# Grams over four banks, a split first substitution and a ranked routing in a delta rule with experts

## The chip, the cores and the metric

One core of a Trainium2 chip runs the whole program. TensorE (PE) multiplies, ScalarE (ACT) and VectorE (DVE) evict PSUM and do elementwise work, GpSimd (POOL) does elementwise work and issues indirect DMAs, SyncE (SP) issues the other DMAs. The metric is the device time of one execution in microseconds (us).

## What is computed

For 4 batches and 8 heads a linear attention with the delta rule runs over 768 tokens with heads of 48; its output, 384 wide per token, goes through a gated layer of 8 experts, one per token, in which a token may keep the expert of the token before it:

```python
for t in range(S):
    kt, vt, bt = (k_n[:, :, t], v[:, :, t], beta[:, :, t, None])
    y[:, :, t] = np.einsum('bhd,bhde->bhe', q[:, :, t], state)
    v_old = np.einsum('bhde,bhd->bhe', state, kt)
    state = state + bt[:, :, :, None] * np.einsum('bhd,bhe->bhde', kt, vt - v_old)
...
    fresh_e = int(np.argmax(logits[b, s]))
    if s == 0 or local_gate[b, s] < 0.5:
        e = fresh_e
    else:
        e = prev_e if prev_e >= 0 else fresh_e
...
    h = np.maximum(x[b, s] @ w1[e], 0.0)
    out[b, s] = p[e] * (h @ w2[e])
```

k_n is the normalised key; the 3072 tokens are spread over the experts by a routing that depends on the data.

## The kernel before

The attention is done in 12 chunks of 64 tokens, n = 0 to 11, two of which make a macro, m = 0 to 5. For each chunk K(n) loads keys and queries (KQ, four DMAs) and multiplies them on TensorE: four products (operand half g, bank c), each into a bank of the two-bank pool pt, each evicted by two ScalarE operations (gt, G) and two of VectorE (gt, amp). For each macro T_(m) transposes gt into L (L218), forms the norms and the factors mu (L220 to L226, one square root on ScalarE), writes mu on the diagonal of X (L231), scales L in two halves (L232) and solves a triangular system by forward substitution: 31 steps j, each of two operations (fg, the product of column j of L with row j of X, L241; X less that, L242) on 31-j rows by j+1 columns. A table SPLIT gives, for each macro, how many columns VectorE does; in the kernel before it is zero everywhere, so all steps run on GpSimd. The result X is transposed to TT (L249) and TX (L252). Per chunk, Tc(n) then makes the matrix XT from TT and TX (two small products through pt, four ScalarE copies), and online(n) does what depends on the state S: kps<-S, R (L288, VectorE), kps<-R,xtp, Us (L300), the new state Sps, S (L307), the output y through yps (ScalarE L312, VectorE L313), its store to xs and its DMA transpose xt, and the logits of 64 tokens (TensorE L326, VectorE L330).

The experts' part begins inside this: the weights of expert 0 are loaded early. A first routing (z=0) takes 20 of 24 pieces of the tokens, up to chunk 9, and gathers a lot of 256 tokens of expert 0; a second (z=1) waits for chunk 11 and completes the positions. Then come expert 0's up- and down-projections for both lots, expert 1, and, in an order written by hand (rest), experts 2 to 7, with weights split in a high and a low f16 part (low part: line 433, method `lo` of weights, L457 to L474). A down-projection (downm, L451) takes 24 matmuls of 384 columns for each tile of up to 128 tokens.

The order of everything up to expert 2 comes from a list scheduler, Sched: each operation has an engine or a choice of engines, a cost, and a rank that is the longest path behind it; `boost` adds to the rank, `links` add a path that isn't a dependence. Operations with `claim` wait for other operations on the same buffer as a whole. What the scheduler puts on an engine runs in that order; an instruction that waits holds up all behind it on its engine.

## Time and profile before

| | |
|---|---|
| median of 3 runs | 582.48 us (582.31 to 582.53) |
| profiled execution | 586.47 us, of which the span 584.8 |
| TensorE busy | 459.1 us, 79% of the span |
| VectorE busy | 329.3 us, 56% |
| GpSimd busy | 285.9 us, 49%, of which the substitution 109.8 + 98.4 |
| ScalarE busy | 210.6 us, 36% |

The shares are means over stages. Up to about 267 us the substitutions run on GpSimd, from about 360 us the experts on TensorE; between them lie the last two chunks and the two routings. The share of the whole span therefore says little about a change; the stretch in which it lies says more. A row of a timeline gives the start, the duration, the engine, the line of the kernel, the operation, its output and inputs, how many instructions the row joins, and in brackets how long the engine was idle before it and who released it.

### The profile page before, as it was taken

The numbers are of one execution on the slowest core, as the hardware profiler recorded it, in microseconds if no ns is written. First come the engines' busy times: TensorE is split into PE (matmuls) and PEld (weight loads), VectorE is DVE, ScalarE is ACT, GpSimd is POOL, SyncE is SP. The second block draws the span as 40 slices with busy tenths as digits, with TensorE's granted clock in tenths as the row PEclk, the third lists the DMA queues.
The fourth block names the chain that finished last, engine by engine and source line by source line (L and its number), as shares of the span: only waits on it lengthen the run. The fifth ranks groups of instructions, "written<-read, shape, count | busy, mean of one in ns | idle before, by whom it ended". The sixth has DMA issues, their size and how long they took to land. (4 is left out here: it accounts for less than half of the span.)

```text
span 584.8 us, 18802 instructions
## 1 busy us (share of the span) xinstructions
PE 459.1 (79%) x8119; PEld 351.9 (60%) x8119; DVE 329.3 (56%) x722; ACT 210.6 (36%) x346; POOL 285.9 (49%) x492
## 2 busy tenths in 40 slices
...
GB/s 224 215 188 1 0 3 58 161 46 129 165 106 106 142 147 165 86 112 57 4 110 244 79 157 94 117 179 48 123 200 126 171 172 174 152 213 151 90 13 25
DMA packets 63668, 69.47 MB, mean 119 GB/s; under 512 B 42931, under 2 KB 54255, under 8 KB 63584
## 3 DMA queue, kind: packets, MB, share of 16 engines
...
HBM read 49.49 MB, written 10.05 MB: 102 GB/s over the span
## 5 line engine op out<-in xcount | busy, mean ns | idle before, releaser
L242 POOL TENSOR_TENSOR X<-X,fg 128x31 f32<-128x31 f32 (+15 forms) x186 | 109.8, 590 | 14.6
L241 POOL TENSOR_TENSOR fg<-L,X 128x31 f32<-128x31 f32 (+15 forms) x186 | 98.4, 529 | 16.0 <-DVE X L231 1.6
L167 PE MATMUL pt<-W 48*64 48x128 f32 x768 | 64.1, 374 | 22.6 <-DVE gt L210 13.6
L167 PEld LDWEIGHTS pt<-W 48*64 48x64 f32 x768 | 55.3, 193 | 27.3 <-DVE gt L210 16.3
L448 PEld LDWEIGHTS <-W 128*128 128x128 f16 x432 | 43.7, 102 | 33.4 <-issue 6.9
L448 PE MATMUL pt<-kv,W 128*128 128x384 f16 (+3 forms) x288 | 61.5, 346 | 0.9 <-DVE ft L450 0.7
L450 DVE TENSOR_SCALAR ft<-pt 128x384 f32<-128x384 f32 (+6 forms) x72 | 40.1, 557 | 22.6 <-ACT W L449 14.6
L167 PE MATMUL pt<-TT,G 32*32 32x32 f32 x768 | 24.3, 229 | 31.8 <-DVE TT L249 30.8
L211 DVE TENSOR_TENSOR amp<-pt,mask 128x256 f32<-128x256 f32 x48 | 20.2, 422 | 50.1 <-ACT gt L208 30.9
L449 ACT ACTIVATE W<-pt 128x256 f16<-128x256 f32 (+4 forms) x28 | 12.2, 437 | 85.5 <-PE pt L448 84.1
L167 PEld LDWEIGHTS pt<-TT,G 32*32 32x32 f32 x768 | 22.5, 139 | 33.0 <-issue 27.2
L433 DVE SCALAR_TENSOR_TENSOR W<-W,W 128x768 f16<-128x768 f32 (+1 forms) x33 | 35.9, 1093 | 10.1 <-ACT W L431 9.9
L455 PEld LDWEIGHTS <-W 128*128 128x128 f16 (+2 forms) x272 | 28.0, 103 | 21.9 <-issue 6.4
...
L436 POOL DMA_INDIRECT G<-xs,gi x25 | 26.6, 1066 | 22.2 <-PE pt L612 12.6
L167 PE MATMUL kps<-R,xtp 64*64 64x48 f32 x704 | 35.6, 281 | 0.7 <-issue 0.7
L449 ACT ACTIVATE xtp<-pt 128x384 f16<-128x384 f32 (+4 forms) x28 | 14.7, 526 | 56.0 <-PE pt L448 43.9
L167 PEld LDWEIGHTS kps<-R,xtp 64*64 64x64 f32 x704 | 34.4, 200 | 0.9 <-issue 0.7
L431 ACT ACTIVATE W<-W 128x768 f16<-128x768 f32 (+1 forms) x33 | 30.2, 935 | 10.7 <-DMA W<-in_moe_w_dram 8.2
L208 ACT ACTIVATE gt<-pt,ma 128x128 f32<-128x128 f32 x48 | 22.4, 479 | 27.1 <-PE pt L167 18.6
...
L455 PEld LDWEIGHTS <-amp 128*128 128x128 f16 (+2 forms) x224 | 22.6, 101 | 14.6 <-issue 0.9
(307 smaller groups left out, 944.1 us busy)
## 6 DMA issues: line engine op xcount, KB each, us to landing
...
G<-xs,gi POOLq DMA_INDIRECT x25
kv<-G SPq DMA_TRANSPOSE x25
```

Of the source, the lines that this page charges most:

```text
L167: mm=lambda o,l,r,st,sp,tp:MM(o,l,r,start=st,stop=sp,skip_group_check=True,tile_position=tp)
L208: add(lambda go=go,gv=gv:nc.scalar.activation(go(),gv()[:,:,0:32],AF.Copy,scale=s.ma[:,0:1]),r=[ps,"mask"],w=[key],claim=[gt],e='A',c=ca(128))
L211: add(lambda gv=gv,n0=n0:nc.vector.tensor_tensor(am.t[:,n0:n0+4,:],gv()[:,:,64:128],s.mask.unsqueeze(1).to_broadcast([128,4,64]),op=ALU.mu ...
L241: eng.tensor_tensor(tv,l[:,j,j+1:].unsqueeze(2).to_broadcast([128,n,k]),x[:,j,x0:x1].unsqueeze(1).to_broadcast([128,n,k]),op=ALU.mult)
L242: eng.tensor_tensor(x[:,j+1:,x0:x1],x[:,j+1:,x0:x1],tv,op=ALU.subtract)
L431: if e in (None,s.nc.scalar): s.nc.scalar.mul(o,i,256.0)
L433: def wlo(s,st,w,k): s.nc.vector.scalar_tensor_tensor(s.wv(w,k)[:,1],s.wst(st,k),256.0,s.wv(w,k)[:,0],op0=ALU.mult,op1=ALU.subtract)
L436: return s.nc.gpsimd.indirect_dma_start(out=x[0:m],out_offset=None,in_=s.xs[0:nt,:],in_offset=bass.IndirectOffsetOnAxis(ap=ix[0:m],axis=0) ...
L448: for k in range(3): s.nc.tensor.matmul(ps,s.wv(W[k],k)[:,a,0,128*f:128*f+128],xT[:,3*b+k,:],start=(x==0 and k==0),stop=(x==2 and k==2))
L449: def uphi(s,h,ps): s.nc.scalar.activation(h,ps,AF.Relu,scale=2.0**-6)
L450: def upt(s,t,ps): s.nc.vector.tensor_scalar(t,ps,0.0,2.0**-6,op0=ALU.max,op1=ALU.mult)
L455: s.nc.tensor.matmul(po[0:m],h(a,f)[:,c:c+m],s.wv(W[k],k)[:,b,f%2,:],start=(x==0 and f==0),stop=(x==2 and f==7))
```

## The change

- SPLIT becomes 4 for macro 0: columns 0 to 3 of its substitution go to VectorE (temporary fv), GpSimd starts at step 4 with columns 4 and up. The costs of the steps and one link of the planner change.
- The grams of chunks 0 and 1 go into kps and yps (two banks each), 16 matmuls in one operation. A one-element GpSimd copy (`held`) waits for chunk 1's keys; the loads of later keys and of all values wait for it.
- The routing's 12 small VectorE constants come behind the scaling of macro 0 in the program.
- Tc copies the lower half of XT in one 128-partition operation, and it and the masked copy may go to VectorE.
- Tc and online of chunk n get a rank raised by 2000 (12-n); grams of later chunks are linked to earlier evictions.
- The first routing gets a rank raised by 20000.
- Low parts 3 to 6 of expert 1's weights are put on GpSimd.
- The last tiles of at most 64 tokens use down2: two halves of 192 columns in two column groups of TensorE.
- L and X tiles join the pool of weight buffers; further costs in the planner change.

```diff
-    NKV=3; NW=15; NAMP=6; NXT=3; NLX=2; NGT=1; NUS=2; SPLIT=(0,0,0,0,0,0)
+    NKV=3; NW=15; NAMP=6; NXT=3; NLX=2; NGT=1; NUS=2; SPLIT=(4,0,0,0,0,0)
...
-        for f,e,c in extra: add(f,e=e,c=c,w=["consts"])
...
+                k1=ch[1]["KQ"][1]; add(lambda:nc.gpsimd.tensor_copy(KQ[0].t[0:1,0,0:1],k1.t[0:1,0,0:1]),r=[k1],w=[KQ[0]],e='G',c=200); s.held=S.ops[-1]
...
+                if n<2:
+                    bb=(s.pkp,s.pyp)[g](); bt_=bb.pool.tiles[0]; pc=[bt_[:,0],bt_[:,1]]
+                    def f(g=g,pc=pc):
                         k=KV(KQ[g].t)
                         for u in range(4):
...
+                            for j,c,q in H: mm(pc[c][B(q),128*u:128*u+128],k[D(j),u,q,0,:],k[D(j),u,q].rearrange("r z t -> r (z t)"),u==0,True,(64*j,64*q))
+                    add(f,r=[KQ[g]],w=[(bb,0),(bb,1)],claim=[bb,gt,am,G2],e='P',c=1300)
...
-                    add(fm,r=[(L,j//16)],w=[(X,p),("fm",p)],claim=[L,X],e='VG'[p],c=400+2.4*n*k if p==0 else 450+3.5*n*k)
+                    add(fm,r=[(L,j//16)],w=[(X,p),("fm",p)],claim=[L,X],e='VG'[p],c=300+3.2*n*k if p==0 else 590+3.85*n*k)
...
+            add(lambda e:(e.copy if e is nc.scalar else e.tensor_copy)(XT.t[:,:,32:64],tt()),r=[TT],w=[(XT,1)],claim=[XT],e='AV',c=dict(A=1070,V=700))
             for q in range(2):
-                o,o2=slice(64*q,64*q+32),slice(64*q+32,64*q+64)
-                add(lambda o2=o2:nc.scalar.copy(XT.t[o2,:,32:64],tt()[o2]),r=[TT],p=[XT],e='A',c=ca(512))
...
+                if m<0:
+                    for f,e,c in extra: add(f,e=e,c=c,w=["consts"]); S.ops[-1].pre.update([s.scaled] if e=='V' else ())
...
+                    i0=len(S.ops); Tc(n); online(n)
+                    for o in S.ops[i0:]: o.boost=2000.*(N-n)
...
+    def down2(s,po,h,W,c,m,y,pv):
+
+        for f in range(8):
+            k=3+f//2
+            for x,(a,b) in enumerate(((0,0),(0,1),(1,0))):
+                for g in range(2):
+                    s.nc.tensor.matmul(po[64*g:64*g+m,0:192],h(a,f)[:,c:c+m],s.wv(W[k],k)[:,b,f%2,192*g:192*g+192],start=(x==0 and f==0),stop=(x==2 and f==7),skip_group_check=True,tile_position=(0,64*g))
+        s.nc.scalar.copy(y[0:m,192:384],po[64:64+m,0:192])
+        s.nc.vector.tensor_scalar(y[0:m,0:192],po[0:m,0:192],pv[0:m],2.0**-26,op0=ALU.mult,op1=ALU.mult)
+        s.nc.vector.tensor_scalar(y[0:m,192:384],y[0:m,192:384],pv[0:m],2.0**-26,op0=ALU.mult,op1=ALU.mult)
...
-            add(lo,r=[CK,w],w=[st],p=[(w,'lo')],claim=[w],e='VG',c=dict(V=cv(n),G=2*cg(n))); S.ops[-1].pre.update(aft[1:] if aft else ())
+            add(lo,r=[CK,w],w=[st],p=[(w,'lo')],claim=[w],e='G' if aft and k>2 else 'VG',c=dict(V=cv(n),G=2*cg(n))); S.ops[-1].pre.update(aft[1:] if aft else ())
...
+            if z==0:
+                for o_ in S.ops[iz_:]: o_.boost=2e4
...
+                if m>64:
+                    s.downm(po,lambda z,f:h(z,f,n),W[e],range(8),128*j,m); s.yo(y,po,s.pv[:,a:a+1],m)
+                else: s.down2(po,lambda z,f:h(z,f,n),W[e],128*j,m,y,s.pv[:,a:a+1])
```

What the planner makes of it is seen at three places. The first is VectorE at the end of macro 1's transposes (L_118 and X_120 belong to macro 1, L_117 and X_119 to macro 0). Before, the mu chain and the scaling of L follow at once:

```order
L218 STREAM_TRANSPOSE L_118<-gt_112 128x256 x4
L220 TENSOR_SCALAR ss_109<-L_118 128x32
L222 RECIPROCAL t_111<-s_110 128x32
L224 TENSOR_TENSOR t_111<-t_111,ss_109 128x32
L224 TENSOR_TENSOR t_111<-t_111,s_110 128x32
L224 TENSOR_SCALAR nn_105<-t_111 128x32
L224 RECIPROCAL mm_108<-nn_105 128x32
L226 TENSOR_TENSOR t_111<-mm_108,bt_104 128x32
L226 TENSOR_TENSOR mm_108<-mm_108,t_111 128x32
L232 TENSOR_TENSOR L_118<-L_118,mm_108 128x512
L231 COPY X_120<-mm_108 128x32
```

After, the same chain is interrupted behind its first operations by the columns of macro 0 (fv), of which the first of 26 steps stand here,

```order
L233 STREAM_TRANSPOSE L_118<-gt_112 128x256 x4
L235 TENSOR_SCALAR ss_109<-L_118 128x32
L256 TENSOR_TENSOR fv<-L_117,X_119 128x104
L257 TENSOR_TENSOR X_119<-X_119,fv 128x26x4
L237 RECIPROCAL t_111<-s_110 128x32
L256 TENSOR_TENSOR fv<-L_117,X_119 128x100
L257 TENSOR_TENSOR X_119<-X_119,fv 128x25x4
```

and goes on only behind the last of them:

```order
L256 TENSOR_TENSOR fv<-L_117,X_119 128x4
L257 TENSOR_TENSOR X_119<-X_119,fv 128x4
L243 STREAM_TRANSPOSE nT_106<-nn_105 128x32
L239 TENSOR_TENSOR t_111<-t_111,ss_109 128x32
L239 TENSOR_TENSOR t_111<-t_111,s_110 128x32
L239 TENSOR_SCALAR nn_105<-t_111 128x32
L239 RECIPROCAL mm_108<-nn_105 128x32
L241 TENSOR_TENSOR t_111<-mm_108,bt_104 128x32
L241 TENSOR_TENSOR mm_108<-mm_108,t_111 128x32
L247 TENSOR_TENSOR L_118<-L_118,mm_108 128x512
L246 COPY X_120<-mm_108 128x32
```

So the scaling of macro 1's L, the last operation here but one, moved behind 52 operations of macro 0.

The second place is VectorE at the end of macro 5 (TT and TX are the transposes of its X, R that of chunk 10, y_135 the output of chunk 9). Before:

```order
L276 TENSOR_TENSOR kv_102<-kv_102,nT_107 128x768
L249 STREAM_TRANSPOSE TT_121<-X_120 128x256 x4
L252 STREAM_TRANSPOSE TX_122<-X_120 128x256 x4
L288 TENSOR_TENSOR R_131<-kv_101,kps 128x768
L313 SCALAR_TENSOR_TENSOR y_135<-yps,y_135 128x2x384
L330 COPY lg<-pt_147 128x18
```

After:

```order
L328 SCALAR_TENSOR_TENSOR y_135<-yps,y_135 128x2x384
L303 TENSOR_TENSOR R_131<-kv_101,kps 128x768
L264 STREAM_TRANSPOSE TT_121<-X_120 128x256 x4
L267 STREAM_TRANSPOSE TX_122<-X_120 128x256 x4
L285 COPY xtp_99<-TT_121 128x16x32
L273 TENSOR_SCALAR xtp_99<-TT_121,ma 128x16x32
L345 COPY lg<-pt_146 128x18
L345 TENSOR_TENSOR lg<-lg,pt_146 128x18
L345 TENSOR_SCALAR lg<-lg 128x18
L536 TENSOR_REDUCE mxl<-lg 128x20
```

R and y moved ahead of the transposes that wait for GpSimd's last step, and the first routing (L536) follows the next logits.

The third place is GpSimd behind its last substitution step (hz and G are gathers of tokens). Before:

```order
L242 TENSOR_TENSOR X_120<-X_120,fg 128x31
L436 DMA hz_128<-xs,gi 128x768
L436 DMA hz_129<-xs,gi 128x768
L657 COPY oh<-oh_209 128x8x20
L657 COPY oh<-oh_211 128x8x4
L661 TENSOR_TENSOR y_135<-oh,ps 128x192
L436 DMA G_113<-xs,gi 128x768
L436 DMA G_114<-xs,gi 128x768
```

After:

```order
L687 COPY oh<-oh_211 128x8x4
L691 TENSOR_TENSOR y_135<-oh,ps 128x192
L499 TENSOR_TENSOR X_120<-X_120,c_168 128x768
L499 TENSOR_TENSOR W_83<-X_120,W_83 128x768
L499 TENSOR_TENSOR W_84<-W_84,c_168 128x768
L499 TENSOR_TENSOR xtp_97<-W_84,xtp_97 128x768
L499 TENSOR_TENSOR xtp_98<-xtp_98,c_168 128x768
L499 TENSOR_TENSOR xtp_99<-xtp_98,xtp_99 128x768
L499 TENSOR_TENSOR amp_91<-amp_91,c_168 128x768
L499 TENSOR_TENSOR amp_92<-amp_91,amp_92 128x768
L454 DMA G_113<-xs,gi 128x768
L454 DMA G_114<-xs,gi 128x768
```

Eight operations on expert 1's weights (L499, 128x768) now stand ahead of the gathers into G.

## Rows read from the trace of the kernel before

**Rows 1.** Busy time of each engine (and its instructions), granted TensorE clock, DMA, by stretch:
```profile
core 0: us, PE busy (x) PEld busy (x) DVE busy (x) ACT busy (x) POOL busy (x), PEclk, DMA share, GB/s
270.00:285.00 15.00, 13.84 (x455) 13.29 (x452) 1.92 (x5) 8.99 (x13) 0.00 (x0) 0.50 0.32 56
315.00:330.00 15.00, 4.49 (x71) 3.52 (x70) 13.51 (x38) 6.22 (x8) 2.15 (x2) 0.50 0.25 86
360.00:570.00 210.00, 201.37 (x1236) 117.60 (x1234) 136.83 (x229) 66.28 (x103) 51.27 (x43) 1.00 0.46 134
```

**Rows 2.** Timeline of GpSimd, ends of macros: start, duration (us), operation, count, [idle <-releaser]:
```profile
28.65 0.52 POOL L241 TENSOR_TENSOR fg<-L,X 128x31 f32<-128x31 f32 x1
...
68.49 0.24 POOL L241 TENSOR_TENSOR fg<-L,X 128x31 f32<-128x31 f32 x1
...
226.20 0.53 POOL L241 TENSOR_TENSOR fg<-L,X 128x31 f32<-128x31 f32 x1 [1.39 <-DVE X L231]
...
267.08 0.25 POOL L242 TENSOR_TENSOR X<-X,fg 128x31 f32<-128x31 f32 x1
```

**Rows 3.** Timeline of GpSimd, single operations of macro 0:
```profile
47.96 0.62 POOL L241 TENSOR_TENSOR fg<-L,X 128x256 f32<-128x256 f32 x1
48.65 0.77 POOL L242 TENSOR_TENSOR X<-X,fg 128x256 f32<-128x256 f32 x1
...
67.85 0.24 POOL L241 TENSOR_TENSOR fg<-L,X 128x31 f32<-128x31 f32 x1
```

**Rows 4.** Timeline of VectorE, constants and mu chain of macro 0:
```profile
24.38 0.18 DVE L395 CAST io<-ib 128x54 f32<-128x54 int32 x1
...
25.88 0.35 DVE L222 RECIPROCAL t<-s 128x32 f32<-128x32 f32 x1
```

**Rows 5.** Timeline of GpSimd and of VectorE where both work in SBUF:
```profile
50.21 1.23 POOL L242 TENSOR_TENSOR X<-X,fg 128x255 f32<-128x255 f32 x1
...
47.90 0.19 DVE L224 TENSOR_TENSOR t<-t,ss 128x32 f32<-128x32 f32 x1
...
50.21 0.69 DVE L232 TENSOR_TENSOR L<-L,mm 128x512 f32<-128x512 f32 x1
```

**Rows 6.** Timelines of ScalarE, VectorE, TensorE and its weight loads around the last macro's end:
```profile
261.85 0.81 ACT L312 ACTIVATE y<-yps 128x768 f16<-128x768 f32 x1 [0.66 <-PE yps L167]
...
267.36 0.45 DVE L249 STREAM_TRANSPOSE TT<-X 128x256 f32<-128x256 f32 x1 [7.25 <-POOL X L242]
...
270.52 0.96 DVE L313 SCALAR_TENSOR_TENSOR y<-yps,y 128x768 f16<-128x768 f32 x1
...
285.63 0.18 DVE L330 COPY lg<-pt 128x18 f32<-128x18 f32 x1 [13.65 <-ACT S L307]
...
307.64 0.18 DVE L330 COPY lg<-pt 128x18 f32<-128x18 f32 x1 [0.87 <-PE pt L612]
...
273.81 1.96 PE L167 MATMUL yps<-S,W 48*64 48x48 f32 x64
...
284.64 0.88 PE L326 MATMUL pt<-wc,xt 128*32 128x18 f16 x48
...
284.64 0.66 PEld L326 LDWEIGHTS <-xt 128*32 128x32 f16 x40
```

**Rows 7.** Timelines of VectorE, GpSimd and TensorE in the routings and expert 0:
```profile
325.35 0.95 DVE L433 SCALAR_TENSOR_TENSOR xtp<-xtp,xtp 128x768 f16<-128x768 f32 x1
...
327.55 1.21 POOL L436 DMA_INDIRECT G<-xs,gi  x1 [12.58 <-PE pt L612]
...
382.86 1.39 POOL L691 TENSOR_TENSOR amp<-ft,amp 128x496 f16<-128x496 f32 x1 [1.90 <-ACT amp L449]
...
330.00 2.08 PE L448 MATMUL pt<-W,W 128*128 128x256 f16 x9 [2.77 <-DVE tq L617]
...
345.83 9.54 PE L455 MATMUL pt<-W,W 128*128 128x384 f16 x48 [1.72 <-ACT W L639]
```

**Rows 8.** Timeline of TensorE in the last tile of expert 3:
```profile
465.87 2.11 PE L455 MATMUL yps<-L,amp 128*64 128x384 f16 x12
```

More of the change, by code (lines that the diff above doesn't have):

```diff
@@ L182, in build @@
         add(wsp,r=["wc0","wc1"],w=["wc"],c=300)
-        for f,e,c in extra: add(f,e=e,c=c,w=["consts"])
-        s.kl={}; ch=[{} for _ in range(N)]; mac=[{} for _ in range(NM)]
+        s.kl={}; s.grams=[]; s.outs=[]; ch=[{} for _ in range(N)]; mac=[{} for _ in range(NM)]
         KV=lambda t:t.rearrange("p (u q z) t -> p u q z t",u=4,q=2)
@@ L190, in K @@
             KQ=C["KQ"]=[s.W(),s.W()]; am=C["am"]=s.amp(); G2=C["G2"]=s.G2()
+            if n==2:
+                k1=ch[1]["KQ"][1]; add(lambda:nc.gpsimd.tensor_copy(KQ[0].t[0:1,0,0:1],k1.t[0:1,0,0:1]),r=[k1],w=[KQ[0]],e='G',c=200); s.held=S.ops[-1]
             for g in range(2):
-                for j in range(2): add(lambda g=g,j=j:nc.sync.dma_start(KQ[g].t[D(j)].rearrange("r a t -> r (a t)"),s.kq_[n,g,j]),p=[KQ[g]],e='S',c=196608); s.kl[n]=S.ops[-1]; S.ops[-1].pre.update([s.kl[1]] if n==2 else ())
+                for j in range(2): add(lambda g=g,j=j:nc.sync.dma_start(KQ[g].t[D(j)].rearrange("r a t -> r (a t)"),s.kq_[n,g,j]),p=[KQ[g]],e='S',c=196608); s.kl[n]=S.ops[-1]; S.ops[-1].pre.update([s.held] if n>1 else ())
             if cc==0:
@@ new lines, in K, with f @@
+                for c in range(2):
+                    n0=8*c+4*g
+                    if n<2: ps=(bb,c); cl=[bb]; gv=lambda v=pc[c]:v.rearrange("p (u t) -> p u t",u=4)
+                    else:
+                        ps=s.pt(); cl=[]; gv=lambda ps=ps:ps.t.rearrange("p (u t) -> p u t",u=4)
+                        def f(g=g,c=c,ps=ps):
+                            k=KV(KQ[g].t)
+                            for u in range(4):
+                                for j in range(2):
+                                    q=j^c; mm(ps.t[B(q),128*u:128*u+128],k[D(j),u,q,0,:],k[D(j),u,q].rearrange("r z t -> r (z t)"),u==0,True,(64*j,64*q))
+                        add(f,r=[KQ[g]],w=[ps],claim=[gt,am,G2],e='P',c=1100); s.grams.append(S.ops[-1])
+                        for o in s.outs[-8:-4]: S.links.append((o,s.grams[-1]))
@@ L232, in fL @@
             def fL(e,z): l=full(L.t)[:,16*z:16*z+16]; e.tensor_mul(l,l,mu.t.unsqueeze(1).to_broadcast([128,16,32]))
-            for z in range(2): add(lambda e,z=z:fL(e,z),r=[mu,ss],w=[(L,z)],claim=[L],**VG(512))
+            for z in range(2): add(lambda e,z=z:fL(e,z),r=[mu,ss],w=[(L,z)],claim=[L],**VG(512)); s.scaled=S.ops[-1]
             for j in range(31):
@@ L341, in build @@
             for i in range(2): pool.init[i]=[o for o in src.bufs[-1].ops]
-        for pool in (s.amp,s.xtp):
+        for pool in (s.L,s.X,s.amp,s.xtp):
             s.W.join(pool,[[o for b in pool.bufs for o in b.ops]]*len(pool.tiles))
@@ L512, in graph @@
             add(lambda eq=eq,sl=sl:V.tensor_reduce(fr[:,sl],eq(),op=ALU.min,axis=AX.X),r=["eq"+Z],w=["fr"+Z],claim=[b2])
-            add(lambda sl=sl:V.scalar_tensor_tensor(rs[:,sl],s.lg[:,sl,E],-1.5*2.0**-23,s.first[:,sl],op0=ALU.is_lt,op1=ALU.max),r=lgk,w=["rs"+Z])
+            add(lambda sl=sl:V.scalar_tensor_tensor(rs[:,sl],s.lg[:,sl,E],-1.5*2.0**-23,s.first[:,sl],op0=ALU.is_lt,op1=ALU.max),r=[*lgk,CK],w=["rs"+Z])
             def fk(kp=kp,sl=sl,n=n):
@@ L603, in graph @@
             add(fv,r=["tb"+Z,"smr"+Z,CK],w=["va"+Z],c=600)
-            r0,r1=(0,SP) if z==0 else (0,NS); nn=r1-r0; obk=[("ob",i) for i in range(0,r1,4)]; oak=["oa0"] if z==0 else ["oa1","oa2"]
+            r0,r1=(0,SP) if z==0 else (0,NS); nn=r1-r0; obk=[("ob",i) for i in [*range(0,SP,4),*range(SP,r1,4)]]; oak=["oa0"] if z==0 else ["oa1","oa2"]
             for part,(c0,c1,vk) in enumerate(((0,3,[]),(3,5,["va0"]+(["va1"] if z else [])))):
@@ L674, in graph @@
         add(lambda:s.oneh(4,8,ta,rhv()),r=["ta","va0","va1",CK],w=[rh],c=900)
-        add(lambda:s.prods(4,8,rhv(),q.t),r=[rh]+[("ob",i) for i in range(0,NS,4)],w=[q],claim=[OB,OB2],e='P',c=24*50)
+        add(lambda:s.prods(4,8,rhv(),q.t),r=[rh]+[("ob",i) for i in [*range(0,SP,4),*range(SP,NS,4)]],w=[q],claim=[OB,OB2],e='P',c=24*50)
         add(lambda:s.finish(4,8,q.t,tq[2]),r=[q],w=["gi2"],c=1500)
```

38 lines of the change are left out of this document (16 added, 22 removed).

## The prediction

> **What bounds the kernel now.** I read the busy time by stretches first, then each engine's timeline at the borders of the stages, asking at each border who was waited for. Three stages with different limits show up. From 28.65 to 267.33 us the bound is GpSimd: it runs the six forward substitutions almost without a gap. Macro 0 starts at 28.65 and macro 1 follows its last operation at 68.49; macro 5 starts at 226.20 after only 1.39 us of waiting for VectorE, and the last operation ends at 267.08 + 0.25 = 267.33 [rows 2]. I call that end P; the reader is to see that six starts and one end are all that this stage needs. From macro 2 on TensorE, ScalarE and VectorE are close behind GpSimd, as the 1.39 shows. After P comes a tail of the last two chunks, two routings and the start of expert 0: TensorE is busy 13.84 of 15 us at a granted clock of 0.50, the 1.2 GHz level (270 to 285), then VectorE 13.51 of 15 (315 to 330). From 360 us the experts run, TensorE 201.37 of 210 us busy at 1.00 [rows 1]: there only TensorE work counts.
>
> **The base.** The profiled execution took 586.47 us (span 584.8, 1.67 outside it); the median of the three runs is 582.48. I sum differences in the profiled execution and take them off the median, as 0.7% of a difference of some 13 us is below 0.1 us.
>
> **Start.** The grams of chunks 0 and 1 go into four other banks, all 16 matmuls of an operation before the first eviction. The evictions still run in turn on ScalarE and VectorE, and claims on the whole buffer keep the evictions of its two banks in one chain. I take 0 for it, bounds -0.5 (the hand-over between groups goes) to +0.8 (a first group twice as long). The twelve constants leave the path: they run from 24.38, and the reciprocal of the mu chain waits until 25.88 [rows 4]; the square root between them, which the chain needs too, is given 0.4, so -1.1. The held loads cost nothing here: those of chunks 0 and 1 are issued first as before. GpSimd's macro 0 starts at 28.65 - 1.1 = about 27.5; I call it t.
>
> **Macro 0 split.** A GpSimd step of 31 elements takes 0.64 (67.85 to 68.49), one of 256 elements 0.62 + 0.77 and two gaps of 0.07, 1.53 [rows 2, 3], so about 0.52 + 0.004 per element. 31 steps on all columns hold 5456 elements; 27 steps on 28 columns hold 3654. That takes off 4 x 0.52 + 1802 x 0.004 = 9.3, and GpSimd ends macro 0 at t + 28 to 30. But GpSimd does not set the start of macro 1 any more. VectorE now has 62 added operations on at most 112 elements; five steps stand between the evictions of chunks 2 and 3, and 26 steps, 52 operations, stand **before** the rest of macro 1's mu chain and the scaling of its L. What is queued behind them is thus the release of macro 1 itself. Free, such an operation takes 0.19 (128x32) [rows 5] plus about 0.05: 52 x 0.24 = 12.5 after the last transposes at t + 18, plus 3 for the chain, and macro 1 would start at t + 33.5 = 61, 7.5 earlier than now. If every column operation has to alternate with a GpSimd operation (0.62 to 0.77 long) as long as GpSimd works, 19 of the 52 fit before t + 29.7, the other 33 take 7.9, the chain 3: t + 40.6 = 68.1, 0.4 earlier. The trace shows both: a GpSimd operation of 255 elements took 1.23 instead of 0.77 beside a VectorE scaling with two SBUF inputs (0.69), while a small one on VectorE took its 0.19 [rows 3, 5]. I lie between, nearer the second, since the operations are of the same two-input kind: macro 1 starts at 66, -2.5.
>
> The Trainium skill, page "SBUF — State Buffer", section "Who interferes with whom", says that a VectorE instruction with two SBUF inputs and a GpSimd instruction that reads SBUF share a port pair as an exclusive lock, the second blocking fully. It speaks against the split; the trace agrees for the long operations (1.23 beside 0.69), and by the rule alone the start of macro 1 would be the 68.1.
>
> Behind the columns stand also half a scaling, two kv products, the twelve constants and the eight transposes of X (2.5), so TensorE's work for chunks 4 and 5 starts some 2 us later than now. Macros 2 to 5 then have to be fed in the same time as before; macro 5 was late by 1.39 already [rows 2]. Fewer, wider copies on ScalarE help, nine of 128x512 and more moved to VectorE hinder. Of the -2.5 I leave -2 at P: 265.3, bounds -7 (no lock) to +3 (the later transposes carried to the end).
>
> **Tail, against P.** The raised ranks of chunks 9 to 11 and of the first routing move three things.
> (1) VectorE does the R of chunk 10 and the y of chunk 9 before the transposes of the last macro. Now these wait: the last transpose stood 7.25 us for GpSimd, y came at 270.52, though ScalarE had its part done at 261.85 + 0.81 [rows 6]. So TensorE does the product S for chunk 10's y (1.96) and a logits group (0.88) before P and not behind it, and the logits of chunk 9 follow right behind P. They came at P + 18.3 (285.63, 13.65 idle before it) and should come at about P + 4.5.
> (2) So the first routing runs beside TensorE's work on chunks 10 and 11. The logits of chunk 11 (307.64, P + 40.3) gain the 2.84 of TensorE work and most of the routing's collisions with R and y: -4.5, bounds -2.8 and -6.
> (3) From there to the second up-projection of expert 0 (330.00, P + 62.7) VectorE is the bound. It loses two low-part operations of expert 1's weights (0.95 each [rows 7]) and leftovers of the first routing: -3.5, bounds 0 and -5. Sum of the tail: -8, bounds -3 to -11.
>
> The price is GpSimd. Eight operations of 128x768 stand ahead of the gathers now. No row has that size; 128x496 took 1.39 [rows 7], which scales to 2.15, and 0.77 at 256 scales to 2.3; for the lower end I take 1.6 by the step's slope. 8 x 1.6 to 2.3 is 13 to 18 us. The last pair also waits for the eviction of the second up-projection (330.00 - 2 - 8 = 320 plus some 4), so the gathers start at 328 to 332, I take 331, where they started at 327.55. The first tokens that they bring to TensorE are those of expert 0's second part; the change has expert 0's first down product ahead of these. It ended at 345.83 + 9.54, 25.4 behind the start of the second up-projection [rows 7], which puts it at 345 to 346. Six gathers at about 1.3 each (1.21 and a gap) have run by 339: hidden, with some 7 us of cover.
>
> **Down products.** Two last tiles (64 and 32 tokens) take 24 matmuls of 384 columns in about 3.9 each: 12 take 2.11 [rows 8], a pitch of 0.163 if the last one's modelled end lies two pitches behind its start. As 48 of 192 columns in two column halves they take half of that if the halves run side by side, the same if not. Logits run in four column groups at 0.88 for 48 [rows 6], 0.018 each, so side by side is what I take: -1.9 each, less 0.4 for the hand-over: -3, bounds 0 and -3.8. Added evictions hide behind the next expert's up-projection. That L and X tiles can now serve as weight buffers, and that copies of Tc may go to VectorE, costs nothing beyond what is priced above.
>
> The Trainium skill, page "TensorEngine Tiling (Array Packing)", section "Restrictions", says column tiling disables Fast Weight Load. By it the halves would be bound by weight loads and the term would be 0; the trace has 40 loads of 32 columns in 0.66 in such groups [rows 6], which speaks against a loss here.
>
> **Sum.** -2 - 8 - 3 = -13: 582.48 - 13 = 569.5.
>
> **Rivals.**
> (a) VectorE's columns run free beside GpSimd: P earlier by 6 to 7 instead of 2, so 564 to 565. For it: the 0.19 in rows 5; against: 1.23 in rows 5.
> (b) The tail gives little: TensorE stays at half clock and is the bound whatever is first, (2) gives 2.8 and (3) nothing, and the split nothing at P: -3 - 3 = 576 to 577. For it: the 13.84 of 15 in rows 1.
> (c) Nothing arrives: P later by 3, the tail -3, the halves 0: 582.5, no change.
> (d) Slower: GpSimd's eight low-part operations delay the gathers. Each us beyond the cover of 7 makes TensorE wait one us. It decides against the change from gathers that start at about 351 (7 of cover and the 13 gained behind 331); stretched by VectorE as in rows 5 (1.23 for 0.77), eight cost 28 and the gathers start at 342, 4 lost; stretched threefold they start past 355: 584 to 588.
>
> **Chances.** Forecast (566 to 574) 0.47; (a) 0.14; (b) and what lies between it and the forecast 0.23; (c) 0.07; (d) 0.09. The range 560.5 to 580.5 leaves out (c), (d) and a little at both ends. A measurement of this kernel tells some 0.2% from no change: faster 0.84, within 0.2% 0.07, slower 0.09.
>
> **What would show it.** In the profile after: macro 1's first GpSimd operation at about 66 (61: rival (a); past 68: the split gave nothing); the last at about 265 (P); column operations on VectorE of 0.2 or of 0.6; y of chunk 9 ahead of the last transposes and its logits 4 to 5 us behind P; chunk 11's logits at P + 36, the second up-projection at P + 54; gathers at P + 64 to 66 and no TensorE wait for them; the last tiles of experts 3 and 4 at about 2 us. Wrong would make it: gathers past 340, a TensorE wait between 320 and 345, or macros 2 to 5 that lose what macro 0 gains.

## The result and the profile after

The changed kernel takes 588.8 us (586.23 to 589.72, 6 runs), the kernel before on the same chip 582.8: a ratio of 1.0087, 95% interval 1.0070 to 1.0105. It is slower by 0.9%; the forecast was 569.5, range 560.5 to 580.5. Three stretches of the profiled execution (588.55, span 586.8) say where that lies, P being the end of the last substitution and E1 the start of expert 1's up-projection on TensorE (368.0 before, 374.0 after):

| | before | after | forecast of the difference |
|---|---|---|---|
| P | 267.33 | 277.62 | -2 |
| P to E1 | 100.7 | 96.4 | -8 |
| E1 to the end of the span | 216.8 | 212.8 | -3 |

The profiled execution of before was 4 us over its median, and nearly all of that is in its second row: two later kernels with its order up to there (down2_only, before_yfirst) show 96.7 and 96.8 instead of 100.7. Against these the tail gained 0.4, and 10 - 0.4 - 4 is the 6 us of the medians. So P is the loss, and the tail gave nothing.

GpSimd in the kernel after, first and last operations of macros and one copy (to be held against [rows 2]):

```profile
25.93 0.23 POOL L256 TENSOR_TENSOR fg<-L,X 128x27 f32<-128x27 f32 x1 [0.44 <-POOL X L246]
...
53.45 0.24 POOL L257 TENSOR_TENSOR X<-X,fg 128x27 f32<-128x27 f32 x1
62.48 0.53 POOL L256 TENSOR_TENSOR fg<-L,X 128x31 f32<-128x31 f32 x1 [8.78 <-DVE X L246]
...
103.05 0.24 POOL L256 TENSOR_TENSOR fg<-L,X 128x31 f32<-128x31 f32 x1
...
147.47 0.76 POOL L246 COPY X<-mm 128x32 f32<-128x32 f32 x1 [12.09 <-DVE mm L241]
...
153.89 0.24 POOL L256 TENSOR_TENSOR fg<-L,X 128x31 f32<-128x31 f32 x1
...
277.37 0.25 POOL L257 TENSOR_TENSOR X<-X,fg 128x31 f32<-128x31 f32 x1
```

Macro 0 starts 2.7 us earlier than before, macro 1 6.0 and macro 2 3.5 earlier (106.5 before). Macro 3 starts 9.1 later (144.8 before). In between, GpSimd stands for 12.09 us in macro 2, at a copy for macro 3 that waits for VectorE's factors. That is visible, and it was in the order of instructions too; the experiments show that without it GpSimd waits elsewhere. In GpSimd's rows the 10.3 us at P add up so: macro 1 starts 6.0 earlier, that copy with its wait takes 12.8, the other waits are 1.4 shorter, and the steps of macros 1 to 5 themselves take 202.0 us where they took 197.1.

VectorE in the kernel after at the end of macro 1 (lg is the logits of chunk 0, TT macro 1's transposes):

```profile
99.20 0.68 DVE L247 TENSOR_TENSOR L<-L,mm 128x512 f32<-128x512 f32 x1
...
101.03 0.91 DVE L328 SCALAR_TENSOR_TENSOR y<-yps,y 128x768 f16<-128x768 f32 x1
108.21 0.18 DVE L345 COPY lg<-pt 128x18 f32<-128x18 f32 x1 [6.28 <-PE pt L341]
...
108.85 1.41 DVE L264 STREAM_TRANSPOSE TT<-X 128x256 f32<-128x256 f32 x4
```

X is complete at 102.97, but the transposes end at 110.26, since the logits stand ahead of them; before they ended at 107.0, 0.5 behind X, with the logits behind. The logits wait for TensorE, which works on chunk 1 from 101.99 on, when y of chunk 0 is evicted: so the transposes now hang on y as well. Waits of TensorE between 90 and 270 us, line and releaser, then us in total, times and the longest; of before:

```profile
PE yps L167 <- DVE y L313: 10.9, 5, 5.7
```

and of after:

```profile
PE yps L167 <- DVE y L328: 23.3, 7, 6.4
```

The bank of y must be evicted by VectorE before the next chunk's chain can start on TensorE, and VectorE has that eviction behind the whole scaling of the next L (three times in the kernel before, four times now). This wait grew by 12.4 us, and P came 12.3 later than forecast; that the two agree is chance, for when the wait is cut by 9.8 us (after_yfirst) P comes only 3.3 earlier.

VectorE, then ScalarE, at the end of macro 5 in the kernel after (to be held against [rows 6]):

```profile
277.32 0.96 DVE L328 SCALAR_TENSOR_TENSOR y<-yps,y 128x768 f16<-128x768 f32 x1 [3.86 <-ACT y L327]
...
279.60 0.95 DVE L303 TENSOR_TENSOR R<-kv,kps 128x768 f32<-128x768 f32 x1 [1.32 <-PE kps L167]
280.47 1.42 DVE L264 STREAM_TRANSPOSE TT<-X 128x256 f32<-128x256 f32 x4
...
285.11 0.18 DVE L345 COPY lg<-pt 128x18 f32<-128x18 f32 x1
```
```profile
276.48 0.81 ACT L327 ACTIVATE y<-yps 128x768 f16<-128x768 f32 x1 [0.19 <-PE yps L167]
```

Chunk 9's y, at 261.85 in [rows 6], is at 276.48 now: the chunks run that much late, so y and R wait, and the transposes behind them end 4.3 us behind P instead of 0.5.

GpSimd, VectorE and TensorE in the routings, kernel after (to be held against [rows 7]):

```profile
325.90 2.44 POOL L499 TENSOR_TENSOR X<-X,c 128x768 f32<-128x768 f32 x1 [5.46 <-ACT W L449]
...
335.20 2.50 POOL L499 TENSOR_TENSOR xtp<-xtp,xtp 128x768 f16<-128x768 f32 x1
345.48 1.47 POOL L499 TENSOR_TENSOR amp<-amp,c 128x768 f32<-128x768 f32 x1 [7.78 <-ACT amp L449]
...
348.88 1.08 POOL L454 DMA_INDIRECT G<-xs,gi  x1
```
```profile
326.93 1.95 DVE L620 TENSOR_TENSOR ob<-ib,ri 128x512 f16<-128x512 int32 x1
328.81 1.59 DVE L612 TENSOR_TENSOR oa<-ib,ri 128x8 f16<-128x8 int32 x1
...
336.33 1.40 DVE L752 SCALAR_TENSOR_TENSOR tq<-tq 128x4 f32<-128x4 f32 x1
```
```profile
340.26 6.40 PE L466 MATMUL pt<-W,W 128*128 128x256 f16 x36 [3.13 <-DVE tq L645]
...
362.07 3.78 PE L466 MATMUL pt<-amp,W 128*128 128x224 f16 x36 [0.73 <-ACT amp L669]
```

An operation of 8 elements takes VectorE 1.59 us beside GpSimd's low parts. The second up-projection starts at 340.26, P + 62.6 where it was P + 62.7, and the gathers into G at 348.88, P + 71.3 where P + 65.7 was forecast. But TensorE hardly waits for what they bring (0.73 at 362.07): the price is paid on VectorE.

### The profile page after: what moved, and what is told of

It is laid out like the page before. It is cut to its first block, busy times and chain, and to the rows that moved or that the text cites. A ratio compares the mean times of both kernels' runs of the same rounds, so it can differ in the third digit from the quotient of the medians.

```text
span 586.8 us, 18939 instructions
## 1 busy us (share of the span) xinstructions
PE 456.2 (78%) x8167; PEld 352.0 (60%) x8167; DVE 355.2 (61%) x787; ACT 188.2 (32%) x328; POOL 297.8 (51%) x496
## 5 line engine op out<-in xcount | busy, mean ns | idle before, releaser
L257 POOL TENSOR_TENSOR X<-X,fg 128x192 f32<-128x192 f32 (+23 forms) x182 | 104.4, 574 | 14.3
L256 POOL TENSOR_TENSOR fg<-L,X 128x192 f32<-128x192 f32 (+23 forms) x182 | 97.5, 535 | 23.2 <-DVE X L246 8.8
L167 PE MATMUL pt<-W 48*64 48x128 f32 x640 | 54.6, 381 | 13.5 <-DVE gt L224 9.4
L473 PEld LDWEIGHTS <-W 128*128 128x128 f16 (+2 forms) x444 | 44.4, 100 | 30.7 <-issue 3.1
L467 ACT ACTIVATE W<-pt 128x384 f16<-128x384 f32 (+5 forms) x48 | 24.1, 502 | 81.5 <-PE pt L466 73.7
L466 PEld LDWEIGHTS <-W 128*128 128x128 f16 x336 | 34.2, 102 | 24.9 <-issue 6.4
L466 PE MATMUL pt<-kv,W 128*128 128x384 f16 (+2 forms) x192 | 43.6, 347 | 0.7 <-DVE ft L468 0.6
L167 PE MATMUL yps<-S,W 48*64 48x48 f32 x704 | 18.5, 276 | 23.8 <-DVE y L328 23.8
L167 PEld LDWEIGHTS yps<-S,W 48*64 48x64 f32 x704 | 16.9, 190 | 25.4 <-DVE y L328 25.2
L466 PE MATMUL pt<-kv,amp 128*128 128x384 f16 (+1 forms) x96 | 28.0, 333 | 0.5 <-DVE ft L468 0.4
L167 PE MATMUL pt<-QQ,TX 32*32 32x32 f32 x768 | 24.5, 228 | 3.2 <-ACT G L223 2.2
L222 ACT ACTIVATE gt<-pt,ma 128x128 f32<-128x128 f32 x40 | 19.2, 485 | 23.3 <-PE pt L167 22.3
L451 DVE SCALAR_TENSOR_TENSOR W<-W,W 128x768 f16<-128x768 f32 (+1 forms) x20 | 22.1, 1107 | 7.3 <-ACT W L449 7.3
```

The source lines that it names most:

```text
L167: mm=lambda o,l,r,st,sp,tp:MM(o,l,r,start=st,stop=sp,skip_group_check=True,tile_position=tp)
L222: add(lambda go=go,gv=gv:nc.scalar.activation(go(),gv()[:,:,0:32],AF.Copy,scale=s.ma[:,0:1]),r=[ps,"mask"],w=[key],claim=[gt,*cl],e='A',c=480)
L256: eng.tensor_tensor(tv,l[:,j,j+1:].unsqueeze(2).to_broadcast([128,n,k]),x[:,j,x0:x1].unsqueeze(1).to_broadcast([128,n,k]),op=ALU.mult)
L257: eng.tensor_tensor(x[:,j+1:,x0:x1],x[:,j+1:,x0:x1],tv,op=ALU.subtract)
L451: def wlo(s,st,w,k): s.nc.vector.scalar_tensor_tensor(s.wv(w,k)[:,1],s.wst(st,k),256.0,s.wv(w,k)[:,0],op0=ALU.mult,op1=ALU.subtract)
L466: for k in range(3): s.nc.tensor.matmul(ps,s.wv(W[k],k)[:,a,0,128*f:128*f+128],xT[:,3*b+k,:],start=(x==0 and k==0),stop=(x==2 and k==2))
```

## The experiments

Two theories ran through them: GpSimd's wait for that copy (or its part in general) sets P; or the chunk loop through TensorE and VectorE does. Ratios are to the kernel before on the same chip.

**xcopy.** The copy that GpSimd waited for goes to VectorE.

```diff
-            if o.takes: o.fn(engines[x])
+            if o.takes: o.fn(engines['V' if o is s.xc else x])
```

> The changed kernel with one instruction moved: the copy of macro 3's mu onto the diagonal of X, which stands on GpSimd between macro 2's steps 26 and 27 and waits 12.1 us there, goes to VectorE behind the first half of the scaling; no other instruction moves. Theory A (the copy holds up GpSimd's queue): GpSimd ends macro 2 at about 141 instead of 153.6, macro 3 starts when its L is scaled, at about 149.3 instead of 153.9, and the end of the substitutions comes 4 to 5 us earlier: 583.5 to 585. Theory B (TensorE, ScalarE and VectorE set the pace behind macro 1 anyway): macro 3 starts earlier but the last substitution ends less than 1 us earlier: 588 to 589.

591.6 us, 1.0103 (1.0056 to 1.0151): no gain. GpSimd in this run at the border of macros 2 and 3:

```profile
140.68 0.25 POOL L257 TENSOR_TENSOR X<-X,fg 128x31 f32<-128x31 f32 x1
149.55 0.53 POOL L256 TENSOR_TENSOR fg<-L,X 128x31 f32<-128x31 f32 x1 [8.62 <-DVE X L246]
```

Macro 2 ends 13 us earlier, macro 3 starts 4 earlier and P comes 1.7 earlier: GpSimd only waits in another place. The copy is not what loses the head start. (The profiled execution is 3.1 us over this run's median, and its excess lies behind P, with E1 at P + 104.3.)

**split0.** The change without its split of macro 0.

```diff
-    ...SPLIT=(4,0,0,0,0,0)
+    ...SPLIT=(0,0,0,0,0,0)
```

> The changed kernel without the split of macro 0 (all columns on GpSimd, the planner orders the rest anew; the copy of mu then stands on VectorE for macros 1 to 5). Theory A: macro 1 starts at about 67 instead of 62.5, but no copy holds up GpSimd, so the substitutions end at about 267 to 270 instead of 277.6: 578 to 582. Rival E (the raised ranks of the chunks cost the time, by putting logits ahead of the transposes of X on VectorE): the end stays at 275 or later: 586 to 592.

594.7 us, 1.0187 (1.0154 to 1.0219), longer than either expectation. P is 274.6 without a split and without GpSimd waiting for a copy, still 7.3 later than before: most of the loss at P belongs to neither. The longer time lies behind P: here TensorE does part of expert 0's first up-projection (319.84) ahead of chunk 11's logits (324.33), and E1 is at P + 105.3.

**down2_only.** The kernel before with the halved down products of the last tiles alone.

```diff
+                else: s.down2(po,lambda z,f:h(z,f,n),W[e],128*j,m,y,s.pv[:,a:a+1])
```

> The kernel before with one part of the change: down-projection in two column halves for the two last tiles of 64 and 32 tokens. Theory D (the halves run side by side): about 2.0 us instead of 3.9 each, 579.0 in all. Rival: the halves run one behind the other, or the added evictions show: 582.5 to 583.5.

579.5 us, 0.9920 (0.9888 to 0.9952). TensorE in the last tile of expert 3, its last 24 of 48 matmuls:

```profile
461.62 1.16 PE L462 MATMUL yps<-L,amp 128*64 128x192 f16 x24
```

The tile runs from 460.60 to 462.70, 2.1 us, where it took 4.0 (463.90 to 467.92, the last half of it in [rows 8]). The halves run side by side.

**lo_back.** The change with the low parts 3 to 6 of expert 1 left to the planner, which puts them on VectorE.

```diff
-e='G' if aft and k>2 else 'VG'
+e='VG'
```

> The changed kernel with the low parts 3 to 6 of expert 1's weights back where the planner puts them (VectorE). Theory C (GpSimd's two-input operations hold VectorE up by the shared port): the VectorE operations between 326 and 337 us, which took 1.4 to 2.5 instead of 0.2 to 1.2 (some 7.6 us more in sum), fall back to their former times, four operations of 0.95 come on top, and the second up-projection of expert 0 starts 3 to 5 us earlier against the end of the substitutions: 584 to 586. Rival: the long operations are long for another reason, or the up-projection waits for something else: the four operations only add, 588 to 592.

580.0 us, 0.9946 (0.9924 to 0.9968). The operations of VectorE that were stretched, and the first gather on GpSimd:

```profile
323.42 0.68 DVE L620 TENSOR_TENSOR ob<-ib,ri 128x512 f16<-128x512 int32 x1
324.02 0.16 DVE L612 TENSOR_TENSOR oa<-ib,ri 128x8 f16<-128x8 int32 x1
```
```profile
327.57 1.20 POOL L454 DMA_INDIRECT G<-xs,gi  x1 [10.65 <-PE pt L640]
```

They take 0.68 and 0.16 instead of 1.95 and 1.59; the second up-projection comes at P + 57.2 instead of 62.6, E1 at P + 90.3 instead of 96.4. Low parts on GpSimd thus cost the tail 6 us in these executions, and some 8 us of the median time. P is 273.65 in this run, with the same order up to macro 5 as after. In the five profiled executions with this order on VectorE it is 273.65 (lo_back), 276.17 (lo_norank), 277.54 (lo_norout), 277.62 (after) and 277.94 (lo_tt5); TensorE's granted clock from 90 to 270 us is 0.68 in lo_back and 0.61 to 0.63 in the other four. So a difference of P between two runs says something only where the clock is similar.

**d_cons_split.** The kernel before with the halved down products, the moved constants, and the split with the change's planner costs and link, nothing else.

```diff
-SPLIT=(0,0,0,0,0,0)
+SPLIT=(4,0,0,0,0,0)
...
-c=400+2.4*n*k if p==0 else 450+3.5*n*k)
+c=300+3.2*n*k if p==0 else 590+3.85*n*k)
...
-                        if j==0 and m: S.links.append((s.lastfm,S.ops[-1]))
+                        if j==0 and m>1: S.links.append((s.lastfm,S.ops[-1]))
```

> The kernel before with three parts of the change: the halved down-projections, the twelve constants behind the scaling, and the split of macro 0 with its planner costs; grams, ranks, copies of Tc and low parts as before. Theory F (the split is good by itself; what the changed kernel lost between macro 2 and 5 came from the new order of the other parts): macro 1 starts at 62 to 63, the substitutions end at 262 to 266, 573 to 577. Rival (the split itself feeds macros 2 to 5 too late, since TensorE starts on chunk 4 no earlier): they end at 267 to 270, 578 to 581.

617.2 us, 1.0529 (1.0488 to 1.0569), outside both expectations. P is 305.7, and the transposes end 9 to 23 us behind their X in every macro; in macro 1, whose X is complete at 116.3, VectorE has a y (124.80) and an R (127.22) ahead of them. The planner's order decides far more than the columns' own time.

**lo_norank**, **lo_norank_link**, **lo_norout.** lo_back without the raised ranks of the chunks; without these and the links from evictions to grams; and lo_back without the raised rank of the first routing alone.

```diff
-                    for o in S.ops[i0:]: o.boost=2000.*(N-n)
+                    for o in S.ops[i0:]: o.boost=0.
...
-                        for o in s.outs[-8:-4]: S.links.append((o,s.grams[-1]))
+                        for o in (): S.links.append((o,s.grams[-1]))
...
-                for o_ in S.ops[iz_:]: o_.boost=2e4
+                for o_ in S.ops[iz_:]: o_.boost=0.
```

> The changed kernel with the low parts back where the planner puts them and without the raised ranks of Tc and online (the links of the grams and the routing's rank stay). Against the kernel with the low parts alone back (580.0; substitutions ended at 273.7). Theory E (the ranks put logits, R and y ahead of the transposes of X and of the grams): the end of the substitutions falls to 266 to 270 and the time to 574 to 577. Rival: no change beyond 2 us; the links or the grams' new evictions make the pace.

> As the run without the raised ranks, and without the links from evictions to the grams of later chunks too; the copy of macro 3 then stands on VectorE. If the links delay the grams, the end of the substitutions falls by another 2 to 5 us against the run without ranks; if not, it stays within 2 us.

> The changed kernel with the low parts back and without the raised rank of the first routing (ranks of the chunks stay). Against the kernel with the low parts alone back (logits of chunk 11 at 38 us behind the end of the substitutions, second up-projection at 57). If the early first routing gives the tail its gain, both come 2 to 5 us later and the time is 581 to 585; if the raised ranks of the chunks and the removed low parts give it, nothing moves by more than 1 us.

lo_norank: 580.4 us, 0.9910 (0.9871 to 0.9950), no different from lo_back. Its VectorE runs in the same order up to P as in lo_back, logits ahead of the transposes included, so the ranks are not what put them there, and what the expectation wanted to test was not changed. lo_norank_link: 588.8, 1.0047 (1.0020 to 1.0074), P 282.9: the links help. lo_norout: 587.7, 1.0019 (0.9983 to 1.0055); E1 is at P + 94.0 instead of 90.3, and the part behind E1 takes 215.5 instead of 211.1: the routing's rank is worth 3.7 us of tail and 4.4 behind it. None of the three makes P earlier than lo_back's.

**lo_xcopy**, **lo_tt5**, **lo_yfirst**, **lo_all.** On lo_back: the copy of xcopy; the last macro's transposes ahead of y of chunk 9 and R of chunk 10 on VectorE; y of the even chunks ahead of the scaling of L; and all three. A move puts the second member and what it depends on ahead of the first in the planner's list:

```diff
-        for o,x in s.order():
+        for o,x in s.ahead(s.order()):
...
+        S.moves=[(ch[9]['y'],mac[5]['tt'])]
...
+        S.moves=[(mac[m+2]['L'],[ch[2*m]['y']]) for m in range(4)]
```

> The changed kernel with the low parts back on VectorE (580.0, run lo_back), and the 32-column copy into macro 3's X on VectorE instead of GpSimd, where it waits 12.1 us between steps of macro 2. Theory G (the held GpSimd is what lost the head start): macro 2 ends on GpSimd near 141 instead of 150.4, macro 3 starts when its L is ready, at 145 to 148 instead of 150.5, P 3 to 5 us earlier than 273.65, the time 575 to 577. Theory K (the chunk loop through TensorE and VectorE sets the pace, and GpSimd only waits elsewhere): macro 2 ends early, but macro 3 starts no earlier than 149 and P moves by less than 2 us.

> The same base, and on VectorE the last macro's transposes (TT and TX) put ahead of the eviction of chunk 9's y and the R of chunk 10, as they stood before the change; nothing else moves. The prediction counted the change's order (y and R first) as part of the gain of the tail. Theory H (it costs, since y and R are not ready at P and the transposes wait for them: TT ends at P+4.6): TT ends at P+1.5 to P+2, lg of chunk 11 and the up products of expert 1 come 2 to 3 us earlier after P (88 instead of 90.3), the time 577. The prediction's step: y and R now come later, the last two logits with them, and the tail gets 1 to 2 us longer.

> The same base, and on VectorE the evictions of the y of chunks 0, 2, 4 and 6 put ahead of the scaling of the L of macros 2 to 5 (behind it, TensorE waited 6.67 us for y at 102.3 and 5.43 us at 146.3 for the chain to go on). Theory K (the chunk loop sets the pace): each y comes 2.5 to 3.5 us earlier, TensorE goes on that much earlier, the L of macros 3 to 5 is ready 2 to 6 us earlier, P 3 to 6 us earlier than 273.65, time 575 to 577. Theory G (GpSimd sets the pace): L of macro 2 to 5 is ready 0.9 us later at macro ends that wait for it, P the same or 1 us later.

> The three edits together. If G, H and K each hold in part, P comes 5 to 9 us earlier than 273.65 (near the 267.3 of the kernel before), the tail 2 us shorter, the time 569 to 575, faster than the kernel before by 1.5 to 2.5%. If neither loop alone sets the pace but TensorE at half clock does, P moves by less than 3 us and the time stays at 577 to 580.

lo_xcopy: 581.8 us, 0.9923 (0.9897 to 0.9949), no gain over lo_back's 0.9946. Macro 2 ends at 141.1, macro 3 starts with its L at 147.0, and each later macro starts with its L; P is 275.0.

lo_tt5: 581.8, 0.9908 (0.9883 to 0.9933). VectorE behind P (277.9 here):

```profile
277.97 0.45 DVE L281 STREAM_TRANSPOSE TT<-X 128x256 f32<-128x256 f32 x1 [1.61 <-POOL X L274]
...
280.32 0.91 DVE L345 SCALAR_TENSOR_TENSOR y<-yps,y 128x768 f16<-128x768 f32 x1
...
285.99 0.18 DVE L362 COPY lg<-pt 128x18 f32<-128x18 f32 x1 [2.79 <-PE pt L358]
```

The transposes end 0.5 behind P, but the logits come at P + 8.1 (lo_back: 7.6) and E1 at P + 91.8 (90.3). The expected gain did not come. The two times do not differ beyond their intervals, so only the profiled executions speak, by 1.5 us, for the prediction's order.

lo_yfirst: 572.4, 0.9753 (0.9705 to 0.9800). VectorE and TensorE at the end of macro 1:

```profile
98.10 0.94 DVE L345 SCALAR_TENSOR_TENSOR y<-yps,y 128x768 f16<-128x768 f32 x1
98.97 0.69 DVE L264 TENSOR_TENSOR L<-L,mm 128x512 f32<-128x512 f32 x1
```
```profile
99.10 1.96 PE L184 MATMUL yps<-S,W 48*64 48x48 f32 x64 [3.28 <-DVE y L345]
```

TensorE goes on at 99.10 instead of 101.99, macro 1's transposes end at 107.2 instead of 110.3, and TensorE's wait for y in the stretch is

```profile
PE yps L184 <- DVE y L345: 13.6, 7, 4.1
```

y and R of the last macro are nearly ready in time, its transposes end at P + 1.7, the logits of chunk 9 come at P + 4.7 and of chunk 11 at P + 34.5, E1 at P + 87.5. The time is 9 us below those of lo_xcopy and lo_tt5 on the same chip. P is 273.7, though, no earlier than lo_back's 273.65, and the L of macro 3 came at 146.8, later than there: those parts of the expectation fell. lo_back's execution had the higher clock (0.68); against those at 0.61 to 0.63 without the move (276.2 to 277.9), lo_yfirst, at 0.63, is 2.4 to 4.2 us earlier.

lo_all: 576.6, 0.9820 (0.9792 to 0.9849), 4.2 us longer than lo_yfirst; P is 272.7, E1 at P + 91.2.

Still open after these was whether y behind L alone makes the loss in the changed kernel, whether it is the change's own, and what held lo_all back.

**after_yfirst**, **before_yfirst**, **lo_yfirst_xcopy.** The y moves in the kernel after, in the kernel before (three of them; the fourth y stands ahead there), and in lo_yfirst with the copy.

```diff
+        S.moves=[(mac[m+2]['L'],[ch[2*m]['y']]) for m in range(4)]
...
+        S.moves=[(mac[m+2]['L'],[ch[2*m]['y']]) for m in range(3)]
```

> The changed kernel with one edit: on VectorE the evictions of the y of chunks 0, 2, 4 and 6 stand ahead of the scaling of the L of macros 2 to 5; all else as it is, the low parts on GpSimd too. Theory K (the planner's new order put four more VectorE operations ahead of y, and TensorE, which waits 23.3 us for y between 90 and 270 us where it waited 10.9, falls behind by that): that wait falls to 13 to 15 us, P comes 3 to 5 us earlier than 277.6, the tail after P is 3 us shorter as well, the time 579 to 582 against 588.8. Rival (the gain of run lo_yfirst needs VectorE's low parts, or was a chip): the time stays within 2 us of 588.8.

> The kernel before with the same edit (y of chunks 0, 2 and 4 ahead of the L of macros 2 to 4; that of chunk 6 stands there already). Theory K1 (the y behind L is a cost that the change brought): before, GpSimd sets the pace and the chunk loop has room, so P stays within 1 us of 267.3 and the time within 1 us of the kernel before. Theory K2 (the chunk loop set the pace before as well, and y behind L was a fault of both kernels): TensorE's wait of 10.9 us falls to 3 to 5, P comes 3 to 5 us earlier, the time falls by 3 to 6 us.

> Run lo_yfirst (572.4) with the copy into macro 3's X on VectorE as well, without the moved transposes that run lo_all had. If the moved transposes were what made lo_all 4 us slower than lo_yfirst, this one stays at 570 to 573; if the copy was (VectorE holds L or the next y back), it comes to 575 to 577 like lo_all.

after_yfirst: 580.6 us, 0.9945 (0.9922 to 0.9968) against 1.0087 for after: four VectorE operations moved give 1.4%, 8 us, and turn slower into faster. TensorE's wait for y falls from 23.3 to 13.5. Its profiled execution is 6 us over its median, so only the stretch up to P, 274.3, is read from it, at a granted clock of 0.67 from 90 to 270 us.

before_yfirst: 582.4, 0.9988 (0.9970 to 1.0006): nothing. P is 267.3, as it was, with TensorE's wait down from 10.9 to 7.5. The same fault stands in the kernel before and costs nothing there; the change took away the room that it had.

lo_yfirst_xcopy: 571.7, 0.9796 (0.9758 to 0.9835), P 272.1, E1 at P + 87.2. In the profiled executions, then, the moved transposes and not the copy held lo_all back, by 4 us of tail; the times cannot tell, since its interval overlaps that of lo_all. This and lo_yfirst beat both kernels, by 2.0 and 2.5% of the kernel before; their intervals overlap. P is 3 us earlier with the move in this pair too (lo_xcopy 275.0).

## Why the prediction was wrong

**Start, and start of macro 1: better, by a mechanism that the prediction had and set aside.** t is 25.93 (27.5), macro 1 starts at 62.48 (66). GpSimd and VectorE in macro 0, with a reciprocal, which has one input, between the columns:

```profile
43.66 0.54 POOL L257 TENSOR_TENSOR X<-X,fg 128x187 f32<-128x187 f32 x1
44.28 0.49 POOL L256 TENSOR_TENSOR fg<-L,X 128x180 f32<-128x180 f32 x1
44.85 0.54 POOL L257 TENSOR_TENSOR X<-X,fg 128x180 f32<-128x180 f32 x1
```
```profile
43.04 0.34 DVE L237 RECIPROCAL t<-s 128x32 f32<-128x32 f32 x1
...
43.73 0.59 DVE L257 TENSOR_TENSOR X<-X,fv 128x100 f32<-128x100 f32 x1
44.35 0.53 DVE L256 TENSOR_TENSOR fv<-L,X 128x96 f32<-128x96 f32 x1
44.92 0.58 DVE L257 TENSOR_TENSOR X<-X,fv 128x96 f32<-128x96 f32 x1
...
55.28 0.20 DVE L256 TENSOR_TENSOR fv<-L,X 128x44 f32<-128x44 f32 x1
...
59.67 0.16 DVE L256 TENSOR_TENSOR fv<-L,X 128x4 f32<-128x4 f32 x1
```

From 42.58 to GpSimd's end at 53.69 the two alternate one for one: each column operation ends 0.08 to 0.12 us behind a GpSimd operation, and the next one of GpSimd starts within 0.05 us of that. That is the prediction's second case, which it put at 68.1 and mixed with the free one. The 0.19 of [rows 5], on which the free one stood, began at 47.90, when GpSimd's operation of 47.20 (0.68 long) had just ended; the next of VectorE, of the same size, began inside one of GpSimd and took 0.49:

```profile
48.13 0.49 DVE L224 TENSOR_TENSOR t<-t,s 128x32 f32<-128x32 f32 x1
```

Mis-sized was the alternation: GpSimd's operations were taken as 0.62 long throughout, but they shrink from 0.59 to 0.24, so that 24 of the 52 fit and not 19; the columns also began at t + 16.4, not t + 18. The Trainium skill, page "SBUF — State Buffer", section "Who interferes with whom", calls the port pair that such operations share an exclusive lock; the alternation here, and the 1.59 us of an 8-element operation beside GpSimd's low parts, agree with it.

**"Of the -2.5 I leave -2 at P, bounds -7 to +3": this step failed; it was +10.3.** It priced the new order by what stands behind the columns on VectorE and let GpSimd go on as the bound. The prediction did name "macros 2 to 5 that lose what macro 0 gains", and read the 1.39 of [rows 2] as the other engines being close behind, but gave it 3 us. What it did not price is that they form a second loop: y evicted, next chunk on TensorE, transposes, products, next L, next y. Before, the L's of macros 2 to 5 were ready at 102.9, 143.6, 183.8 and 226.7 against ends of the macro ahead on GpSimd of 106.5, 144.7, 183.2 and 224.8: from macro 3 on two loops within 2 us of each other, of which [rows 2] show one. The change brought a fourth y behind its L, and chunk 0's logits, which wait for y, stand ahead of macro 1's transposes (110.3, not 107.0). Without the waiting copy (lo_xcopy) every macro from 3 on starts with its L, so the second loop is the later one. Moving the four y gives 8 us of time (after_yfirst), and nothing in the kernel before (before_yfirst). Of these 8 some 3 are seen at P, at a similar clock, and some 3 between P and E1 (lo_back and lo_yfirst); the rest was not placed.

The other part of that step is GpSimd itself, which the prediction let run as fast as before. Its steps stretch beside operations of VectorE that have two inputs in SBUF. The first subtraction of macro 1, beside VectorE's kv product, took 0.86, where it took 0.27 before:

```profile
63.09 0.86 POOL L257 TENSOR_TENSOR X<-X,fg 128x31 f32<-128x31 f32 x1
```
```profile
62.83 0.99 DVE L291 TENSOR_TENSOR kv<-kv,nT 128x768 f32<-128x768 f32 x1
```

The steps of macro 1 took 2.5 us more than before, which is that much of its head start of 6.0; those of macros 1 to 5 together took 4.9 more. What each operation of VectorE has in that was not separated.

Not settled is the rest of P: 272 to 274 in the best runs, not 267. In lo_yfirst_xcopy against before_yfirst macro 1 starts 5.9 us earlier, GpSimd's waits at the later macros are 6.9 longer and its steps take 3.8 more, which makes the +4.8 there; why L still comes late is open. The new order of the grams and the copies of Tc that may go to VectorE were not run alone, and TensorE's clock is another possible cause. Busy time and granted clock of the engines from 90 to 270 us in before:

```profile
90.00:270.00 180.00, 149.28 (x5059) 142.84 (x5053) 101.69 (x222) 91.53 (x148) 154.43 (x275) 0.71 0.48 115
```

and in lo_yfirst:

```profile
90.00:270.00 180.00, 158.00 (x4828) 150.68 (x4828) 97.98 (x217) 70.98 (x128) 150.96 (x262) 0.63 0.48 115
```

TensorE is busy 8.7 us more at a lower granted clock (0.63, 0.71 before), nearer the 1.2 GHz level; that could make L late, but no run changed the clock alone.

**Tail (1): the order is right, its premise was not.** It took y of chunk 9 as ready 5 us ahead of P, from [rows 6]. With the chunks late it came behind P, and so did the transposes. With the chunks in time (lo_yfirst) the logits come at P + 4.7, the predicted P + 4.5, and in the profiled executions of lo_tt5 and lo_all the other order costs 1.5 to 4 us of tail.

**Tail (2): -4.5 was -2.6** (chunk 11's logits at P + 37.7), and -5.8 with the chunks in time (lo_yfirst, P + 34.5).

**Tail (3) and the price: the wrong place.** VectorE was to lose two low parts and gain 3.5; from chunk 11's logits to the second up-projection it took 24.9 us instead of 22.4, since GpSimd's eight operations stretched what was left. With the low parts back on VectorE (lo_back) it is 19.1, a gain of 3.3: the term came without the move that was to bring it. The prediction had the stretching of one engine by the other in a rival, (d), but let it act through the gathers: these came at P + 71.3, behind the P + 65.7 of the forecast and ahead of the P + 76.7 of (d) (342, with P forecast at 265.3), the last pair having waited 7.78 us for ScalarE, and TensorE hardly waited for them. Rival (d)'s 584 to 588 is near the result for a partly other reason; two thirds of the miss lie ahead of P.

**Down products: right.** -3 forecast, bounds 0 and -3.8; the last tile of expert 3 went from 4.0 to 2.1, and the part behind E1 is 4.0 shorter, just past the bound. The Trainium skill, page "TensorEngine Tiling (Array Packing)", section "Restrictions", states that column tiling disables Fast Weight Load; the 0 that the prediction worked out from that as a rival did not come for these tiles.

With both faults mended, the y behind L and the low parts on GpSimd, the kernel is at 571.7 to 572.4, near the 569.5 forecast; that is luck, for it is another sum: of lo_yfirst_xcopy against before_yfirst, P +4.8, the tail -9.6, the rest -5.0.
